# A windowed attention and a two-layer MLP on one core: the first batch taken in two parts of its tokens, the first chunk's first layer in halves, and a new order of all steps

## The chip, the core and the metric

The kernel runs on one core of one Trainium2 chip, as one program. The metric is the time on the device in microseconds (us), the median of several runs. The engines are named as the profile names them: PE (TensorE, matrix products and transposes), PEld (its weight loads), DVE (VectorE), ACT (ScalarE), POOL (GpSimd) and SP (SyncE). Each engine executes its own queue of instructions in order, and waits at an instruction until what that instruction needs is there.

## The reference

```python
# q, k, v: 8 batches x 8 heads x 576 tokens x 64, f32
scores = (1 / 8) * q @ k.transpose(0, 1, 3, 2)
rel = pos[:, None] - pos[None, :]
scores = where((rel >= 0) & (rel < 64), scores, -1e9)     # each query sees 64 keys
attn = softmax(scores)                                    # over the keys
x = (attn @ v).transpose(0, 2, 1, 3).reshape(4608, 512)   # tokens x (heads*64)
h = x @ w_in                                              # w_in 512 x 2048
g = h - tanh(h)
out = g @ w_out                                           # w_out 2048 x 512, out f32
```

## The kernel before

All products are in bf16 with sums in f32 in PSUM, which has 8 banks of 512 f32 columns over 128 partitions.

**Attention.** It is done by batch and pair of heads: pair g = 4 b + pr holds heads pr and pr + 4 of batch b. For the first batches q and k are loaded so that partition p of 96 holds tokens 6p to 6p+5 (L110). A load by POOL's queue casts to bf16 on the way; a load by SP's queue brings f32, which a cast (`ck`, `cq`, L90 on ACT) makes bf16. For each pair PE transposes k and q into a PSUM bank, in 12 matmuls of 96 columns each (`Fp` and `Ep`; L256 for batch 0, L260 for later batches) and a copy (`Fc`, `Ec`, L90 or L92) puts them into `kT` and `qp`. Scores are made for windows of 64 queries against 128 keys, in two groups of five and four windows (`Rp`, with L281 and L286 for batch 0), followed by the exponential (`Rx`, L318). For batch 0 the mask is added by PE before the scores, as a product of the identity with a tile `hide`; later pairs multiply the exponentials by a mask instead (`M`, L323 on DVE). The products with V (`P` and `PP`, L335 for batch 0) have a 65th column that gives the sums, and DVE's norm (`D`, `DS`, `DH`, and for later batches `DR`, `DN`; L377 is one of its lines) divides by them. V is held in tiles of 128 keys; the odd tiles are loaded (`LV` for batch 0, L145, and `lv`, `lt` for batch 1), the even ones are put together from halves of the odd ones by copies (`zr`, `za`, `zb`). The normalised x is turned by PE transposes (`Xp`, L397, with a copy `Xc`) or later by a DMA into chunks of 512 tokens; there are 9 chunks of tokens.

**The MLP.** Chunk c has a first layer of 16 tiles m of 128 hidden units (`H.c.m`, four matmuls of 512 columns, L431; `Hp` does some of its columns, L508), a tanh for each (`A`, L439 on ACT), the subtraction h - tanh(h) for each (`G`, L445 on DVE), and a second layer for each 128 tokens s of the chunk, in four parts of four matmuls (`W.c.s.part`, L474 and L467), with a copy and an output DMA (`O`). w_in is loaded in five blocks (`wi.0` to `wi.4`, L188) and w_out in four (`wo`), all by POOL's queue.

**Order.** Nothing is scheduled by a framework: the string `PLAN` lists all steps, and `play` runs through it word by word, so the queue of each engine has the order of the words in the string. `Fp.2.6` is "transposes of k of pair 2 into bank 6"; a last letter p, s, a or v names POOL, SP, ACT or DVE, as the engine that issues a load or executes a copy. `U.n.bank` (L227) is one filler: matmuls on a tile of constants that no result uses; 35 of them are in the string, each of 512 columns, or 384 in bank 7. `h` makes the tile `hide` and `i` the identity, both on POOL; `mt`, `mv`, `mk`, `mz` set the constant parts of tiles, and `n` and `N` make the mask and put it into PSUM.

## Time and profile before

| | |
|---|---|
| median of 3 runs | 307.93 us (307.8 to 308.22) |
| span of the profiled execution | 305.2 us |
| PE busy | 297.8 us, 98% of the span, 2599 instructions |
| DVE busy | 176.2 us, 58% |
| ACT busy | 157.5 us, 52% |
| POOL busy | 103.7 us, 34% |

The profile is of one execution, and its own time is given as its span: from the first to the last instruction that it shows. The median of the timed runs is 2.7 us longer. Rows of the timeline give the start of an instruction in us from the start of the span, its length, its engine, its line, what it writes and reads, its shape and how many like it follow. Rows of the groups give the line, the engine, the operation, the number, then busy us and mean ns of one, then the idle time of the engine just before them and what ended most of it. Rows of the DMA issues give what is loaded, the queue, the size of one and the median time from issue to landing.

### The profile page before, as it was taken

The numbers are of one execution on the slowest core, as the hardware profiler recorded it, in microseconds if no ns is written. First come the engines' busy times: TensorE is split into PE (matmuls) and PEld (weight loads), VectorE is DVE, ScalarE is ACT, GpSimd is POOL, SyncE is SP. The second block draws the span as 40 slices with busy tenths as digits, with TensorE's granted clock in tenths as the row PEclk, the third lists the DMA queues.
The fourth block names the chain that finished last, engine by engine and source line by source line (L and its number), as shares of the span: only waits on it lengthen the run. The fifth ranks groups of instructions, "written<-read, shape, count | busy, mean of one in ns | idle before, by whom it ended". The sixth has DMA issues, their size and how long they took to land.

```text
span 305.2 us, 6469 instructions
## 1 busy us (share of the span) xinstructions
PE 297.8 (98%) x2599; PEld 149.4 (49%) x2632; DVE 176.2 (58%) x316; ACT 157.5 (52%) x265; POOL 103.7 (34%) x141
## 2 busy tenths in 40 slices
...
GB/s 155 159 195 193 195 207 180 159 205 102 102 143 127 173 125 181 182 108 131 164 177 127 135 173 142 95 143 35 37 76 74 0 69 37 34 34 37 52 51 104
DMA packets 132878, 36.77 MB, mean 120 GB/s; under 512 B 119920, under 2 KB 127344, under 8 KB 132848
## 3 DMA queue, kind: packets, MB, share of 16 engines
q0 software_dynamic: 92752, 18.06, 85.3%
...
## 4 chain that ended last, share of the span: by engine, by line
PE 87%; DVE 5%; ACT 3%; issue 2%; POOL 2%; DVEq 0%; ACTq 0%; POOLq 0%
PE ps L474 38%; PE ps L431 30%; PE ps L508 6%; PE ps L348 3%; PE ps L304 2%; DVE gT L445 2%; PE ps L397 1%; ACT th L439 1%; PE ps L286 1%; PE ps L467 1%; DVE pt L323 1%; PE ps L260 1%; PE ps L281 1%; PE ps L227 1%; POOL qall L110 1%
## 5 line engine op out<-in xcount | busy, mean ns | idle before, releaser
L445 DVE TENSOR_TENSOR gT<-ps,th 128x512 bf16<-128x512 f32 x144 | 97.2, 687 | 85.3 <-ACT th L439 84.6
L474 PE MATMUL ps<-w_out_sb,gT 128*128 128x512 bf16 x527 | 131.5, 380 | 2.2 <-issue 0.8
L439 ACT ACTIVATE th<-ps 128x512 f32<-128x512 f32 x144 | 84.7, 599 | 93.0 <-PE ps L431 79.7
L431 PE MATMUL ps<-xT,wi 128*128 128x512 bf16 x496 | 120.7, 380 | 0.1
L474 PEld LDWEIGHTS <-gT 128*128 128x128 bf16 x560 | 53.3, 98 | 61.4
L431 PEld LDWEIGHTS <-wi 128*128 128x128 bf16 x496 | 47.0, 98 | 54.3
L145 POOL DMA_DIRECT2D vw<-in_v_dram x35 | 30.0, 872 | 36.1 <-PE ps L348 33.5
L90 ACT ACTIVATE ysb<-ps 128x512 f32<-128x512 f32 (+1 forms) x24 | 14.2, 593 | 30.9 <-PE ps L474 30.2
L166 POOL DMA_DIRECT2D qall<-in_q_dram x25 | 21.7, 881 | 24.1 <-DMA qw<-qall 21.4
L166 POOL DMA_DIRECT2D kall<-in_k_dram x25 | 21.7, 875 | 10.4 <-DMA kw<-kall 4.8
L314 ACT ACTIVATE pt<-ps 128x1024 bf16<-128x1024 f32 (+1 forms) x30 | 23.3, 816 | 3.5 <-PE ps L304 3.2
L323 DVE TENSOR_TENSOR pt<-pt,ps 128x1152 bf16<-128x1152 bf16 x28 | 20.5, 749 | 5.1 <-ACT pt L314 3.2
L508 PE MATMUL ps<-xT,wi 128*128 128x512 bf16 x80 | 20.8, 380 | 0.0
L92 DVE COPY ysb<-ps 128x512 f32<-128x512 f32 (+1 forms) x11 | 7.1, 650 | 20.5 <-PE ps L467 13.2
L368 DVE TENSOR_TENSOR xs<-ps,rcp 128x384 bf16<-128x384 f32 x28 | 15.2, 550 | 0.3
L318 ACT ACTIVATE pt<-ps 128x640 bf16<-128x640 f32 (+1 forms) x24 | 14.7, 659 | 0.8 <-PE ps L286 0.8
L348 PEld LDWEIGHTS <-pt 128*64 128x64 bf16 x504 | 9.4, 112 | 6.3 <-DVE pt L323 2.1
L90 ACT ACTIVATE kt<-ps 128x576 bf16<-128x576 bf16 x10 | 6.5, 647 | 10.8 <-PE ps L256 6.8
L227 PE MATMUL ps<-warm 128*128 128x512 bf16 (+1 forms) x35 | 10.6, 435 | 1.1 <-DVE warm L207 1.1
L508 PEld LDWEIGHTS <-wi 128*128 128x128 bf16 x80 | 7.4, 98 | 8.5 <-issue 0.4
L348 PE MATMUL ps<-vw,pt 128*64 128x65 bf16 x504 | 11.0, 197 | 0.3 <-DVE pt L323 0.2
L365 DVE TENSOR_TENSOR xs<-ps,rcp 128x384 bf16<-128x384 f32 x14 | 7.7, 550 | 0.1
...
## 6 DMA issues: line engine op xcount, KB each, us to landing
out_dram<-ysb SPq DMA_DIRECT2D x33, 256.0 KB, 3.1
...
kall<-in_k_dram POOLq DMA_DIRECT2D x11, 144.0 KB, 6.3
qall<-in_q_dram POOLq DMA_DIRECT2D x11, 144.0 KB, 6.6
...
```

The source lines that it names most:

```text
L90: nc.scalar.activation(o, i, ACT.Copy)
L145: nc.gpsimd.dma_start(out=w[:, 2 * i + 1, :, 0:D] if i < NF else w[64:128, 2 * i, :, 0:D], in_=v[b, :, 128 * i:128 * i + n].rearrange("h p ...
L166: nc.gpsimd.dma_start(out=token_rows(b, n)[0:c, i], in_=(q if n == "q" else k)[b, :, 128 * i:128 * i + c].rearrange("h p d -> p h d"))
L314: nc.scalar.activation(o, sp, ACT.Exp, scale=scale)
L323: nc.vector.tensor_tensor(p, p, mask.unsqueeze(1).to_broadcast([128, 2 * NJ, 64]), ALU.mult)
L348: nc.tensor.matmul(ps[r, bank, 65 * i:65 * i + 65], PT[(g + r2) % NPT][:, j, r], vw[b % 2][:, j, p0 + r2 + NP * h, :], start=True, stop=True)
L368: nc.vector.tensor_tensor(xs[b % 2][:, p0 // 2, 0:6, n // 2, :], ov[:, :, 0:D], sums[g][:, n].to_broadcast([128, 6, D]), ALU.mult)
L431: nc.tensor.matmul(hp, w_in_tile(ki, m), chunk_tile(c)[:, n.start // 64:n.stop // 64, ki % 2, 64 * (ki // 2):64 * (ki // 2) + 64], start=( ...
L439: nc.scalar.activation(th[:, n], hp, ACT.Tanh)
L445: nc.vector.tensor_tensor(gT[c][:, m, columns(s)], hp, th, ALU.subtract)
L474: nc.tensor.matmul(yp, gT[c][:, m, s * 128:(s + 1) * 128], w_out_sb[:, m, :], start=n == 1 and i == 0, stop=n == 4 and i == 3)
L508: nc.tensor.matmul(hp, w_in_tile(half + 2 * i, m), chunk_tile(c)[:, :, half, 64 * i:64 * i + 64], start=n == 1 and i == 0, stop=n == 2 and ...
```

## The change

Computation and results are meant to be the same. What differs:

- `kT` and `qp` of a pair become two halves of one tile `kq`, so that one copy (`pc`) can fill both.
- q and k of batch 0 are no longer loaded by pair, but by even pairs (0, 2) or odd pairs (1, 3) and by part of the tokens: part 0 is the first 48 partitions' worth (288 tokens), part 1 the rest, put into partitions 64 to 111. `la` loads k and `lb` loads q. Part 0 of the even pairs comes by SP in f32 and is cast (`ca`, `cb`, on ACT and DVE); the other six loads go by POOL's queue.
- Transposes (`ta`, `tb`) are by part: 12 matmuls of 48 columns. Scores (`ra`), exponentials (`rx`) and the products with V (`pp`) are by part too, part 0 being windows 0 to 3 and part 1 windows 4 to 8. The norm `pd` scales two pairs in one instruction.
- q and k of batch 1 are loaded for two pairs at a time (`l2` for k, `l3` for q), 288 KB each.
- The even tiles of V for batch 0 are put together by two copies (`zl`, `zh`) that can be placed apart.
- The first layer of chunk 0 goes in halves of 256 tokens (`I`, the "duo"): two tiles m share one bank, 8 matmuls of 256 columns, then one tanh (`J`) and one subtraction (`K`) of 512 columns for both.
- The filler is 30 matmuls instead of 35, 23 of 512 columns and 7 of 384, and none of it stands behind the first layer's start.
- There are 576 products with V instead of 584.
- The whole of `PLAN` is in a new order.

The diff, with both orders cut to their beginnings:

```diff
@@ -70,9 +70,10 @@
     vw = [const.tile([128, NJ, H, D + 1], BF16, name=f"vw{i}") for i in range(2)]
     PT_all = const.tile([128, NPT, NJ, 128], BF16, name="pt")
     PT = [PT_all[:, i] for i in range(NPT)]
-    kT = [const.tile([128, 64 + S], BF16, name=f"kt{i}") for i in range(NKR)]
+    kq = [const.tile([128, 2, 64 + S], BF16, name=f"kq{i}") for i in range(NKR)]
+    kT = [t[:, 0] for t in kq]
     kw = [const.tile([128, NP, 64 + S], BF16, name=f"kw{i}") for i in range(2)]
-    qp = [const.tile([128, S], BF16, name=f"qp{i}") for i in range(NKR)]
+    qp = [t[:, 1, 64:] for t in kq]
     qw = [const.tile([128, NP, S], BF16, name=f"qw{i}") for i in range(2)]
     q8 = [const.tile([128, NP, 64], BF16, name=f"q8{i}") for i in range(2)]
     rows_all = {n: [const.tile([128, H, E * D], BF16, name=f"{n}all{i}") for i in range(2)] for n in "qk"}
@@ -110,6 +111,95 @@
         eng.dma_start(out=t, in_=(q if n == "q" else k)[b, pr::NP].rearrange("h (p e) d -> p h (e d)", e=E))
         stage[g, n] = t
+    PART = slice(0, 48), slice(64, 112)
+    def part_source(n, odd, part):
+        src = (q if n == "q" else k)[0, odd::2].rearrange("h (p e) d -> p h (e d)", e=E)
+        return src[48 * part:48 * part + 48]
+    early = []
+    def load_part(n, odd, part, eng):
+        if eng is nc.gpsimd:
+            eng.dma_start(out=rows_all[n][0][PART[part], odd::2], in_=part_source(n, odd, part))
+            return
+        if not early:
+            t = g_pool.tile([128, M, TOK], BF16, tag="gT", name="early")
+            t = t.rearrange("p m t -> p (m t)").bitcast(F32)[:, 0:2 * 4 * E * D]
+            early.append(t.rearrange("p (n h f) -> p n h f", n=2, h=4))
+        t = early[0][PART[part], "kq".index(n)]
+        eng.dma_start(out=t, in_=part_source(n, odd, part))
+    def cast_part(n, g, part, eng):
+        t = early[0][PART[part], "kq".index(n)]
+        move(eng, rows_all[n][0][PART[part], g::NP], t[:, g // 2::2])
+    def load_two(g, n):
+        b, pr = divmod(g, NP)
+        t = rows_all[n][b % 2][0:P]
+        nc.gpsimd.dma_start(out=t[:, pr::2], in_=(q if n == "q" else k)[b, pr::2].rearrange("h (p e) d -> p h (e d)", e=E))
+        for i in range(2):
+            stage[g + 2 * i, n] = t[:, pr + 2 * i::NP]
+    def part_bank(bank):
+        t = ps[:, bank, :].bitcast(BF16)[:, 0:640].rearrange("c (n x) -> c n x", n=2)[:, :, 0:E * 48]
+        return t.rearrange("c n (e p) -> c n e p", e=E)
+    def tr_part(g, n, part, bank):
+        tp, src, r = part_bank(bank)[:, "kq".index(n)], rows_all[n][0], PART[part]
+        for e in range(E):
+            for h in range(2):
+                nc.tensor.transpose(tp[64 * h:64 * h + 64, e, :], src[r, g + NP * h, 64 * e:64 * e + 64], ident[r, r])
+    def put_part(g, part, bank, eng):
+        lo = 64 + 6 * 48 * part
+        move(eng, kq[g][:, :, lo:lo + E * 48].rearrange("c n (p e) -> c n p e", e=E),
+             part_bank(bank).rearrange("c n e p -> c n p e"))
+    def part_group(part, bank):
+        n = 4 + part
+        pair = ps[:, 4:8:3, 0:64 * n] if bank == 4 else ps[:, bank:bank + 2, 0:64 * n]
+        return pair.rearrange("p h (i t) -> p i h t", t=64), range(4 * part, 4 * part + n)
+    def scores_part(g, part, bank):
+        sp, js = part_group(part, bank)
+        n = len(js)
+        for h in range(2):
+            nc.tensor.matmul(sp[:, :, h], ident, hide[:, h].unsqueeze(1).to_broadcast([128, n, 64]),
+                             start=True, stop=False)
+        for i, j in enumerate(js):
+            for h in range(2):
+                r = slice(64 * h, 64 * h + 64)
+                nc.tensor.matmul(sp[:, i, h], kT[g][r, 64 * j:64 * j + 128], qp[g][r, 64 * j:64 * j + 64],
+                                 start=False, stop=i == n - 1)
+    def probs_part(g, part, bank):
+        sp, js = part_group(part, bank)
+        nc.scalar.activation(PT[g][:, js[0]:js[0] + len(js), :].rearrange("p i (h t) -> p i h t", h=2), sp,
+                             ACT.Exp, scale=scale)
+    def two_banks(bank):
+        return (4, 7) if bank == 4 else (bank, bank + 1)
+    def pv_part(g, part, bank):
+        for i in range(4 + part):
+            j = 4 * part + i
+            for h in range(2):
+                r = slice(64 * h, 64 * h + 64)
+                nc.tensor.matmul(ps[r, two_banks(bank)[g % 2], 65 * i:65 * i + 65], PT[g][:, j, r],
+                                 vw[0][:, j, g + NP * h, :], start=True, stop=True)
+    def norm_part(half, part, bank):
+        n = 4 + part
+        ov = ps[:, 4:8:3] if bank == 4 else ps[:, bank:bank + 2]
+        ov = ov[:, :, 0:n * (D + 1)].rearrange("p r (i c) -> p r i c", c=D + 1)
+        rc = sm_pool.tile([128, 2, 5, 1], F32, tag="rc", name="rc")
+        nc.vector.reciprocal(rc[:, :, 0:n], ov[:, :, :, D:D + 1])
+        nc.vector.tensor_tensor(xs[0][:, half, 4 * part:4 * part + n].rearrange("p w r d -> p r w d"),
+                                ov[:, :, :, 0:D], rc[:, :, 0:n].to_broadcast([128, 2, n, D]), ALU.mult)
     def load_all(b, n):
         t = rows_all[n][b % 2][0:P]
@@ -155,6 +245,12 @@
         w = vw[b % 2]
         move(eng, w[0:64, 2 * i + 2], w[64:128, 2 * i + 1])
         move(eng, w[64:128, 2 * i], w[0:64, 2 * i + 1])
+    def low_tile(i, eng):
+        move(eng, vw[0][0:64, 2 * i + 2], vw[0][64:128, 2 * i + 1])
+    def high_tile(i, eng):
+        move(eng, vw[0][64:128, 2 * i], vw[0][0:64, 2 * i + 1])
     def token_rows(b, n="k"):
         t = rows_all[n][b % 2].rearrange("p h f -> p (h f)")[:, 0:(NF + 1) * H * D]
@@ -443,6 +539,27 @@
         if c not in gT:
             gT[c] = g_pool.tile([128, M, TOK], BF16, tag="gT", name="gT")
         nc.vector.tensor_tensor(gT[c][:, m, columns(s)], hp, th, ALU.subtract)
+    def duo_mm(mp, s, bank):
+        n = columns(s)
+        hp = ps[:, bank, :].rearrange("p (m t) -> p m t", m=2)
+        for i in range(2):
+            for ki in range(4):
+                nc.tensor.matmul(hp[:, i], w_in_tile(ki, 2 * mp + i),
+                                 chunk_tile(0)[:, n.start // 64:n.stop // 64, ki % 2, 64 * (ki // 2):64 * (ki // 2) + 64],
+                                 start=(ki == 0), stop=(ki == 3))
+        hidden["duo", mp, s] = hp
+    def duo_tanh(mp, s):
+        th = sm_pool.tile([128, TOK], F32, tag="th", name="th").rearrange("p (m t) -> p m t", m=2)
+        nc.scalar.activation(th, hidden["duo", mp, s], ACT.Tanh)
+        hidden["duo", mp, s] = hidden["duo", mp, s], th
+    def duo_sub(mp, s):
+        if 0 not in gT:
+            gT[0] = g_pool.tile([128, M, TOK], BF16, tag="gT", name="gT")
+        hp, th = hidden.pop(("duo", mp, s))
+        nc.vector.tensor_tensor(gT[0][:, 2 * mp:2 * mp + 2, columns(s)], hp, th, ALU.subtract)
     def yp_bank(c, s):
         return (0, 2)[s % 2] if c == NC - 1 else (2, 0)[s % 2] if c == 0 else 2
@@ -527,6 +644,12 @@
         Fc=lambda g, k, e: put(g, "k", k, e), Ec=lambda g, k, e: put(g, "c", k, e),
         Rp=scores, Rx=probs, M=masking, za=cross_low, zb=cross_high, Z=cross_rows, zr=cross_tile,
         P=pv, D=norm, DS=norm_sums, DH=norm_half, PP=pv_pairs, DR=recip_pairs, DN=norm_pairs, Xp=x_tr, Xc=x_put, Y=x_dma,
+        la=lambda h, p, e: load_part("k", h, p, e), lb=lambda h, p, e: load_part("q", h, p, e),
+        ca=lambda g, p, e: cast_part("k", g, p, e), cb=lambda g, p, e: cast_part("q", g, p, e),
+        l2=lambda g: load_two(g, "k"), l3=lambda g: load_two(g, "q"),
+        ta=lambda g, p, k: tr_part(g, "k", p, k), tb=lambda g, p, k: tr_part(g, "q", p, k), pc=put_part,
+        ra=scores_part, rx=probs_part, pp=pv_part, pd=norm_part, zl=low_tile, zh=high_tile,
+        I=duo_mm, J=duo_tanh, K=duo_sub,
         H=first_layer, Hp=first_layer_part, A=tanh, G=subtract, W=yp_mm, O=y_out)
     def play(script):
@@ -535,89 +658,90 @@
             STEPS[what](*[ENG[a] if a in ENG else int(a) for a in args])
     PLAN = """
-        u mv.0 mv.1 lk.1.p lq.2.p LV.0.2 U.1.3 U.1.3 U.1.5 U.1.7 U.1.6 lk.3.p U.1.1 U.1.7 lk.2.p U.1.7 lq.1.p
-        lq.3.p U.4.3 LV.0.0 i lk.0.s lq.0.s U.1.3 U.1.2 U.4.0 LV.0.3 U.4.0 Ep.2.3 Fp.1.5 U.1.2 Ec.2.3.v zr.0.2.v
-        Fc.1.5.a ck.0.a mt.3 mt.1 U.1.1 U.1.3 U.1.2 U.1.4 mt.2 U.1.1 U.1.4 cq.0.a Fp.0.1 Fp.2.6 Ep.0.2 LV.0.1
-        Ep.1.3 U.1.7 Fp.3.5 Fc.2.6.a LV.0.4 lk.4.p lq.4.p h Ec.0.2.a Fc.3.5.a Ep.3.7 Ec.3.7.a Ec.1.3.v mt.0
-        Fc.0.1.v Rp.1.0.3 lk.5.p Rp.3.0.1 Rx.1.0.3 Rp.0.1.5 zr.0.3.v Rx.3.0.1 zr.0.0.v zr.0.1.v Rp.1.1.4
-        Rp.3.1.0 ck.4.v Rx.0.1.5 Rx.1.1.4 Rx.3.1.0 lq.5.p Rp.0.0.2 wi.1 wi.0 lq.6.p P.1 lv.1.1.0 lk.7.p D.1
-        Rx.0.0.2 cq.4.v Rp.2.1.0 Rp.2.0.3 Rx.2.1.0 P.0 Rx.2.0.3 P.2 Fp.4.2 ck.5.a Fc.4.2.a D.0 Ep.4.4 DS.2 P.3
-        U.1.3 lk.6.p DH.2.0 Ec.4.4.a wi.2 Xp.0.0.1.2 Fp.5.0 Xp.0.0.0.3 D.3 lv.1.0.1 lk.8.p lq.7.p U.1.4 DH.2.1
-        Xc.0.0.0.3.v Rp.4.1.5 U.1.1 lv.1.1.1 Xc.0.0.1.2.v Xp.0.1.0.7 cq.5.a Xp.0.1.1.1 Ep.5.3 Fc.5.0.a
-        Xc.0.1.1.1.v Rx.4.1.5 Hp.0.0.0 mz Xc.0.1.0.7.a ck.7.a Ec.5.3.v Hp.0.2.1 Hp.0.0.1 Rp.4.0.6 Rp.5.1.3 n
-        Hp.0.1.0 U.1.5 Hp.0.2.0 Hp.0.1.1 cq.6.v ck.6.v A.0.0 Ep.6.5 Rx.5.1.3 Rx.4.0.6 G.0.0 lv.1.0.0 A.0.2 A.0.1
-        G.0.2 wi.3 H.0.3 A.0.3 G.0.1 N U.1.7 G.0.3 lq.8.p Fp.6.3 cq.7.v Fp.7.7 Ec.6.5.a H.0.4 ck.8.a H.0.6
-        Fc.7.7.v lt.1 Fc.6.3.a A.0.4 A.0.6 H.0.5 wi.4 A.0.5 Rp.6.1.3 Rp.6.0.6 lq.9.p Rx.6.1.3 Ep.7.5 G.0.4
-        lv.1.3.1 zb.1.1.p lv.1.2.1 H.0.7 G.0.5 G.0.6 za.1.0.v Rp.5.0.3 Rx.6.0.6 A.0.7 H.0.8 H.0.9 zb.1.0.p wo.0
-        Rx.5.0.3 A.0.8 G.0.7 H.0.10 M.6 G.0.8 Ec.7.5.a A.0.9 H.0.11 za.1.1.p lv.1.3.0 A.0.10 M.5 lv.1.2.0 Fp.8.7
-        cq.8.v G.0.9 G.0.10 Rp.7.1.3 A.0.11 wo.2 Fc.8.7.a G.0.11 Rp.7.0.5 H.0.12 lk.9.p Rx.7.0.5 A.0.12 Ep.8.1
...
+        u U.6.3 U.5.4 lb.1.1.p la.1.1.p lb.0.0.s cb.2.0.a mt.2 mt.1 mz la.0.0.s ca.2.0.a mv.0 mv.1 mk cb.0.0.v i
+        lb.1.0.p lb.0.1.p mt.3 mt.0 ca.0.0.v U.1.7 U.2.0 U.1.7 ta.2.0.1 U.1.7 ta.0.0.4 U.1.5 tb.1.1.0 U.1.7
+        la.1.0.p la.0.1.p tb.0.0.4 tb.2.0.1 pc.0.0.4.a LV.0.0 LV.0.1 h U.2.7 ta.1.1.0 tb.1.0.7 tb.3.1.2 U.1.5
+        ra.0.0.5 tb.0.1.4 rx.0.0.5 pc.2.0.1.v pc.1.1.0.v LV.0.2 LV.0.3 l3.4 LV.0.4 U.1.0 tb.3.0.0 tb.2.1.3
+        ta.3.1.2 pc.3.1.2.a U.2.6 ta.1.0.7 ta.0.1.4 ta.3.0.0 ta.2.1.3 ra.2.0.1 pc.1.0.7.a wi.2 zh.1.p pc.2.1.3.v
+        zl.0.v zh.0.a pc.3.0.0.a rx.2.0.1 U.2.5 pc.0.1.4.v ra.1.0.5 rx.1.0.5 U.3.3 ra.1.1.3 rx.1.1.3 wi.0
+        pp.0.0.6 pp.1.0.6 zl.2.v zh.2.v zl.1.v pd.0.0.6 zl.3.v l2.4 cq.6.v pp.2.0.0 ra.3.0.1 ra.0.1.3 rx.3.0.1
+        wi.3 zh.3.p cq.4.p wi.1 wi.4 l2.5 rx.0.1.3 ra.3.1.5 U.1.7 pp.3.0.0 rx.3.1.5 pd.1.0.0 ra.2.1.3 pp.1.1.1
+        Xp.0.0.0.5 Ep.6.7 l3.5 n ck.4.p ck.6.p wo.2 wo.0 rx.2.1.3 Xc.0.0.0.5.a Xp.0.1.0.0 pp.0.1.1 pp.3.1.3
+        pp.2.1.3 Xc.0.1.0.0.a Ep.4.5 I.3.0.0 pd.0.1.1 I.2.0.2 Ec.4.5.a Ec.6.7.a J.3.0 J.2.0 pd.1.1.3 Xp.0.1.1.7
+        Xp.0.0.1.1 Xc.0.0.1.1.a K.3.0 Xc.0.1.1.7.v K.2.0 I.0.0.5 I.0.1.6 Fp.4.2 I.2.1.7 Fp.6.1 I.5.1.3 I.5.0.0
+        J.0.1 Fc.4.2.a K.0.1 Fc.6.1.v J.0.0 J.2.1 K.2.1 I.1.1.6 I.3.1.1 J.5.1 J.5.0 K.5.0 K.0.0 J.3.1 J.1.1
+        K.5.1 I.1.0.0 I.7.1.2 I.6.0.5 Rp.6.0.4 I.4.0.3 J.7.1 Rx.6.0.4 K.1.1 K.3.1 J.6.0 wo.1 wo.3 lv.1.3.0
+        cq.7.p lv.1.2.0 lv.1.1.1 lv.1.0.1 lv.1.0.0 lv.1.1.0 ck.7.v K.7.1 cq.5.v ck.5.v K.6.0 lk.10.p lt.1
+        lv.1.3.1 lv.1.2.1 Rp.6.1.1 Rx.6.1.1 J.1.0 K.1.0 I.6.1.4 J.4.0 K.4.0 Ep.5.2 J.6.1 Ec.5.2.a I.7.0.6
+        Rp.4.1.0 Fp.5.7 Fp.7.5 Rx.4.1.0 Fc.5.7.v K.6.1 Ep.7.3 W.0.0.2 N I.4.1.1 Ec.7.3.a J.7.0 K.7.0 Fc.7.5.v
+        W.0.1.2 Rp.5.0.4 Rx.5.0.4 Rp.7.0.5 W.0.1.0 Rp.4.0.3 W.0.0.0 J.4.1 Rx.4.0.3 Rx.7.0.5 W.0.1.1 Rp.7.1.4
+        Rp.5.1.5 W.0.0.1 W.0.0.3 W.0.1.3 Rx.5.1.5 O.0.0.a Rx.7.1.4 ck.10.a O.0.1.a za.1.3.a za.1.2.a lq.8.p
+        lk.8.p lk.9.p lk.11.p lq.9.p M.6 M.4 M.5 K.4.1 M.7 zb.1.3.p zb.1.2.p lq.11.p lq.10.p cq.8.p W.0.2.1
+        W.0.2.3 W.0.2.2 zb.1.1.v za.1.0.v za.1.1.v zb.1.0.v PP.4 DR.4 DN.4.2 DN.4.1 DN.4.0 Fp.10.1 W.0.3.0
+        W.0.2.0 PP.6 W.0.3.1 Xp.1.0.0.4 Xp.1.0.1.3 W.0.3.3 ck.8.a O.0.2.a Xc.1.0.0.4.a Fc.10.1.v DR.6 DN.6.0
+        DN.6.2 DN.6.1 Xc.1.0.1.3.a Xp.1.1.0.7 Fp.8.4 Xc.1.1.0.7.a LV.2.0 LV.2.3 LV.2.1 cq.9.p LV.2.2 Xp.1.1.1.6
+        Hp.1.1.0 Ep.8.3 Ec.8.3.a Hp.1.0.0 ck.11.v ck.9.v Xc.1.1.1.6.v Hp.1.0.1 A.1.0 Fc.8.4.v cq.11.v G.1.0
+        Hp.1.1.1 Rp.8.1.5 Rx.8.1.5 A.1.1 Fp.11.3 Fc.11.3.v cq.10.v G.1.1 W.0.3.2 H.1.3 lr.3.4 LV.3.3 lr.4.3
...
+        Fp.9.4 Ep.11.5 Ec.11.5.v G.1.3 Ep.9.6 Ep.10.7 Hp.1.2.1 Hp.1.2.0 Fc.9.4.a Ec.10.7.a Ec.9.6.v A.1.2 G.1.2
+        Z.2 Rp.10.1.2 Rp.8.0.4 H.1.6 Rx.8.0.4 Rx.10.1.2 A.1.6 G.1.6 Rp.9.0.5 Rp.11.1.4 Rx.9.0.5 H.1.5 A.1.5
+        G.1.5 H.1.4 Rp.9.1.5 A.1.4 Rx.9.1.5 Rx.11.1.4 M.8 M.9 H.1.9 H.1.8 Rp.11.0.3 PP.8 G.1.4 H.1.7 A.1.9
+        Rx.11.0.3 A.1.8 A.1.7 G.1.9 DR.8 G.1.8 DN.8.0 G.1.7 DN.8.1 DN.8.2 H.1.12 H.1.11 H.1.10 A.1.12 A.1.11
...
```

## The prediction

> **What bounds the kernel now.** I read the page first, then busy time by stretch, then the timeline of the first 23 us.

> ```profile
> span 305.2 us, 6469 instructions
> PE 297.8 (98%) x2599; PEld 149.4 (49%) x2632; DVE 176.2 (58%) x316; ACT 157.5 (52%) x265; POOL 103.7 (34%) x141
> 0.00:7.50 7.50, 6.44 (x22) 2.57 (x22) 1.33 (x5) 1.28 (x1) 6.27 (x14) 1.00 0.99 155
> 7.50:22.58 15.08, 14.63 (x315) 9.86 (x315) 10.84 (x30) 13.14 (x22) 13.23 (x22) 1.00 1.69 176
> 22.58:60.00 37.42, 37.19 (x382) 19.34 (x383) 24.13 (x49) 27.85 (x50) 28.94 (x42) 1.00 1.65 188
> 60.00:302.00 242.00, 239.54 (x1887) 117.68 (x1915) 139.68 (x233) 115.23 (x193) 55.29 (x66) 1.00 1.09 106
> ```

> The rows by stretch give the length, then busy us (and instructions) of PE, weight loads, DVE, ACT, POOL, then PE's clock, DMA share and GB/s. From 22.58 to 302 PE idles only 0.23 + 2.46 = 2.7 us. So a change of order there can win little and lose much; what can be won lies ahead of 22.58, where the first layer begins, and PE's busy time there is partly filler:

> ```profile
> 1.06 4.38 PE L227 MATMUL ps<-warm 128*128 128x512 bf16 x12 [1.06 <-DVE warm L207]
> 7.70 0.45 PE L256 MATMUL ps<-ident,qall 96*64 96x96 bf16 x12
> 7.95 0.45 PE L256 MATMUL ps<-ident,kall 96*64 96x96 bf16 x12
> 8.33 1.90 PE L227 MATMUL ps<-warm 128*128 128x512 bf16 x7
> 22.58 0.38 PE L508 MATMUL ps<-xT,wi 128*128 128x512 bf16 x1
> 57.18 1.73 PE ps L474 x8
> ```

> L227 is the filler (U); all 22 matmuls of the first stretch above are of it. In steady state one 512-column matmul takes 1.73 / 8 = 0.216 us; the first twelve fillers take 4.38. Filler ahead of 22.58 costs 6.44 (22 of them) + 1.74 (seven, 8.33 to 10.07) + about 1.0 (four single ones) = 9.2 us; two more, 0.4 by the steady row, follow. All of this is against the span, 305.2; the median of the runs, 307.93, is 2.7 longer, which lies around the span and which I leave as it is.

> **PE's own work ahead of the first layer.** A record's length holds about 0.17 of pipeline, so I take distances between starts:

> ```profile
> 13.13 0.43 PE L281 MATMUL ps<-hide,ident 128*128 128x320 bf16 x2
> 13.79 0.39 PE L281 MATMUL ps<-hide,ident 128*128 128x256 bf16 x2
> 14.11 0.29 PE L286 MATMUL ps<-qp,kt 64*128 64x64 bf16 x8
> 14.33 0.39 PE L281 MATMUL ps<-hide,ident 128*128 128x256 bf16 x2
> 18.98 0.43 PE L260 MATMUL ps<-ident,kb 96*128 96x96 bf16 x6
> 19.24 0.42 PE L260 MATMUL ps<-ident,qb 96*128 96x96 bf16 x6
> 19.59 0.51 PE L335 MATMUL ps<-vw,pt 128*64 128x65 bf16 x20
> 20.04 0.39 PE L227 MATMUL ps<-warm 128*128 128x512 bf16 x1
> 20.26 0.44 PE L397 MATMUL ps<-ident,xs 128*128 128x128 bf16 x5
> 20.54 0.42 PE L260 MATMUL ps<-ident,kb 96*128 96x96 bf16 x6
> ```

> Transposes of one tensor of one pair: 0.25 (7.70 to 7.95) or 0.26; scores of five windows 0.66 (13.13 to 13.79), of four 0.54 (13.79 to 14.33); twenty products with V 0.45; five transposes of x 0.28.

> Before, up to 22.58: 12 transpose groups of 0.26 (3.1), scores 4 x 1.20 and one group of a later pair, some 0.3 (5.1), 80 products (1.8), 18 transposes of x (1.0), together 11.0; with filler 9.2 and the start at 1.06 that is 21.3, so 1.3 of waits.

> After, up to the first duo matmul: the same scores (4.8), 72 products (1.6), 8 transposes of x (0.45), two groups of batch 1 (0.52), and 16 groups of 12 transposes of 48 columns. Half the columns could give half of 0.25, or each could cost the full 0.25 if loading weights sets it; no row has this size. I take 0.165, nearer to the half, since in the 0.25 rows pairs of transposes run side by side and columns set the distance: 2.6, between 2.0 and 4.0. Sum 10.0. Filler: eleven at the start (4.0 by the row of twelve), then 12 x 0.216 + 7 x 0.162 = 3.7; none afterwards. So 1.06 + 7.7 + 10.0 = 18.8 us without a wait.

> **When its inputs are there.** Two loads go by SP, all others by POOL's queue, in order:

> ```profile
> 1.28 0.43 SPq L110 DMA_DIRECT2D qf<-in_q_dram  x1
> qf<-in_q_dram SPq DMA_DIRECT2D x1, 288.0 KB, 3.7
> kall<-in_k_dram POOLq DMA_DIRECT2D x1, 144.0 KB, 4.9
> 1.80:4.40 2.60, 2.60 (x8) 1.06 (x7) 0.80 (x3) 0.29 (x1) 2.60 (x5) 1.00 0.99 244
> 15.30:26.20 10.90, 10.61 (x213) 6.91 (x212) 8.62 (x24) 9.86 (x17) 9.29 (x15) 1.00 1.42 195
> 10.71 0.65 POOL L110 DMA_DIRECT2D qall<-in_q_dram  x1
> qall<-in_q_dram POOLq DMA_DIRECT2D x1, 144.0 KB, 6.2
> 13.51 1.52 POOL L188 DMA_DIRECT2D wi<-in_moe_w_in_dram  x2
> wi<-in_moe_w_in_dram POOLq DMA_DIRECT2D x1, 256.0 KB, 5.8
> ```

> The load issued at 10.71 landed at 16.9, when eight q/k loads of 144 KB and V's 576 KB had come by POOL: 1728 KB. The first w_in block, issued at 13.51, landed at 19.3, after 2272 KB. In the new order the first-layer block wi.2 ends 2240 KB of POOL's loads and the batch-1 load l3.4 ends 1664 with V's tail still behind it. So wi.2 should land near 19.2 and l3.4 near 16.4. The bytes are the same; what comes forward is the identity matrix (POOL made it after eight issues, now after two) and the first 48 rows of the even pairs, so that transposes start at about 5.9 (second f32 load at 1.28 + 3.7 = 5.0, then a cast of 0.84), not 7.70. POOL gets three more casts and two V copies ahead of the w_out loads, and waits for V in the copies. Some 0.6 to 0.9 us each, they hide under the loads then in flight (wi.2, wi.0, l2.4, wi.3: 1.5 MB, over 7 us at 195 GB/s); without that cover w_out would come up to 3 us later.

> The third chain is ACT's, which makes the exps and most copies out of PSUM:

> ```profile
> 9.11 0.84 ACT L90 ACTIVATE kb<-kf 96x768 bf16<-96x768 f32 x1
> L92 POOL COPY vw<-vw 64x520 bf16<-64x520 bf16 x4 | 2.5, 620 | 2.3 <-DMA vw<-in_v_dram 2.2
> 11.46 0.65 ACT L90 ACTIVATE qp<-ps 128x576 bf16<-128x576 bf16 x1
> 13.37 3.50 ACT L318 ACTIVATE pt<-ps 128x640 bf16<-128x640 f32 x6
> 18.61 0.82 DVE L377 TENSOR_TENSOR xs<-ps,rc 128x640 bf16<-128x640 f32 x1
> 22.26 0.60 ACT L90 ACTIVATE xT<-ps 128x512 bf16<-128x512 bf16 x1
> ```

> After the two casts (to 5.9) ACT can begin pc.0.0 at about 7.4, when q of the first part is transposed. Up to the second x copy it has four copies of 0.65, one V copy (0.65 on ACT at most, by its copies of 576), eight exps of 0.58 and two x copies of 0.6: 9.1 us, so 16.5 without waits. It does wait: for the first scores about 1.5 (PE transposes the odd heads first, and POOL makes the hide mask after two V loads), for the transposes of pairs 3 and 1 about 0.5, for the scores of pair 3, which stand on PE behind three pairs' products with V, about 0.7, and for DVE's scaling pd.1.0.0 about 0.6. The copy zh.0.a waits for V's first block with a copy and seven exps behind it; 992 KB into POOL's queue, the block should be in near 12, when ACT comes to it. That gives 19.8. The two-pair scaling itself costs no more per element than 0.82 for 640, so I price it at zero; its price is that pair 0 waits for pair 1, and that lies in these waits.

> So 18.8 (PE), 19.2 (wi.2) and 19.8 (ACT and DVE) nearly coincide. I take **19.8, with 18.9 to 21.5** as bounds: 2.8 earlier than 22.58.

> **What follows the first layer's start.** Before has done more by its start: two pairs' transposes (1.04 against the 0.52 of after, whose other half is owed), one score group (0.3) and ten more transposes of x (0.55): after owes 1.3 more. It saves the later filler, 0.4. The duo steps stream the same columns: 128 of 256 for 64 of 512. No row has 256 columns with a full weight load of its own outside a change of shape; L281's 0.32 for two (13.79 to 14.11) would add 0.05 each, 6.7 us, but contains that change; the x transposes load 128 weights for every 0.055 us, so the load is covered under 128 columns already. I take zero. The chunk keeps 16 tanh and 16 subtractions, since a duo puts two output tiles of half a chunk into one bank.

> Against this, the new order leaves DVE less room in chunk 1: all of H.1.3 to H.1.15, some 17 us of PE, now run together with four masks, two scalings and the V copies. Before, the same stretch looked like this:

> ```profile
> 70.00:75.00 5.00, 5.00 (x47) 2.48 (x44) 4.81 (x9) 3.58 (x7) 0.00 (x0) 1.00 0.59 107
> L445 DVE TENSOR_TENSOR gT<-ps,th 128x512 bf16<-128x512 f32 x144 | 97.2, 687 | 85.3 <-ACT th L439 84.6
> L323 DVE TENSOR_TENSOR pt<-pt,ps 128x1152 bf16<-128x1152 bf16 x28 | 20.5, 749 | 5.1 <-ACT pt L314 3.2
> ```

> DVE was full (4.81 of 5) and PE lost nothing. Now 14 subtractions (9.6) and four masks (3.0) make 12.6 of 17 us, and the reciprocals, scalings, a copy out of PSUM and V's copies come on top, so DVE is as full as PE. I charge 0.6 for waits there and in chunk 0, between 0 and 2.5 (the whole margin of a DVE that falls one mask and two subtractions behind). From 75 us on the work is the same in another order, with little to win of 2.5 us.

> Sum: -2.8 + 1.3 - 0.4 + 0.6 = -1.3. Forecast **306.6 us**, by itself 305.3 to 307.3.

> [...] The first f32 loads moved 244 GB/s over 96 partitions, ramp included. [...]

> **Rivals.** *A load in DVE's way (slower).* The cast cq.6.v stands on DVE ahead of pd.1.0.0; it waits for l3.4, which the first layer does not need, and pd.1.0.0, its x copy and the first duo stand behind it. At 16.4 it hides (pd.1.0.0 cannot start before about 17.3). Each us of landing beyond 17.3 is a us of the end; past 19.2 the kernel is slower. L3.4 is twice as large as any q/k load of POOL before, and V's short rows lie in front of it; landing at 20.2 gives 306.6 + 2.9 = 309.5. POOL issues it near 11, so it would have to take over 8 us, where 144 KB took 4.9 to 6.2. For it: that size. Against: the count of KB. 0.18.

> *The head start is handed back.* ACT and DVE, in order, stop PE in chunks 0 and 1 by 1.9 instead of 0.6: 307.9. For it: a DVE as full as PE, and in-order copies that wait for loads. Against: before ran so at no loss. 0.18, half of it no change, half slower.

> *Narrow loads.* [...] 0.07.

> *No waits at all.* The first duo at 18.9 with no loss later: -3.7 + 0.9 = -2.8, 305.1. 0.11.

> The forecast keeps 0.46. The range, 304.6 to 309.8, leaves out some 0.06 below and 0.10 above. A measurement here can tell about 0.2%, 0.6 us. Faster by more: 0.40 of the forecast, 0.11, 0.04 of the narrow loads: 0.55. Slower: 0.18 and half of 0.18, with a little of the rest: 0.28. Same: 0.17.

> **What would show it.** Right: first transposes near 5.9, first 256-column matmul at 19 to 20.5, no filler after it, PE idle from there to 80 us under 1.5 us. Wrong: a DVE wait on q of batch 1 ahead of the scaling; the f32 loads landing past 5.6; 256-column matmuls more than 0.11 apart; PE waiting on DVE masks ahead of the products of pairs 8 and 10; the first 48-column groups at 0.25.

## The result, and the profile after

The changed kernel takes 323.08 us (median of 4 runs, 321.42 to 324.5) against 307.87 (4 runs, 307.8 to 308.22): a ratio of 1.049, with a 95% interval of 1.045 to 1.0531. The forecast was 306.6, with 304.6 to 309.8 as range: the sign was wrong and the time lies 13.3 us above the range. The spans of the profiled executions are 322.4 and 305.2. Of the four executions two ran at a mean clock of 0.984 (321.42 and 322.08 us) and two at 0.974 (324.09 and 324.5); the profile is of the one at 324.09. Each ratio here leaves out executions over 1.5% above the fastest of their kernel; the medians are of all.

The page of the changed kernel: span, busy times, and the clock in 40 slices.

```profile
span 322.4 us, 6783 instructions
...
PE 306.5 (95%) x2755; PEld 158.7 (49%) x2791; DVE 182.8 (57%) x320; ACT 150.2 (47%) x253; POOL 107.6 (33%) x146
...
PEclk9559979999999999999999999999999999999999
```

Busy time by stretch of the changed kernel, the columns as in the prediction:

```profile
0.00:9.60 9.60, 7.30 (x54) 3.03 (x54) 3.24 (x15) 2.97 (x3) 8.22 (x19) 1.00 1.05 147
9.60:23.24 13.64, 13.64 (x240) 7.30 (x236) 4.79 (x9) 5.62 (x9) 10.82 (x18) 0.50 1.97 180
23.24:43.70 20.46, 18.64 (x264) 15.25 (x263) 13.52 (x27) 13.31 (x24) 11.27 (x16) 1.00 1.34 200
43.70:47.10 3.40, 3.40 (x29) 2.30 (x26) 1.83 (x3) 2.22 (x5) 2.79 (x5) 0.50 1.31 87
...
28.00:300.00 272.00, 261.37 (x2255) 135.56 (x2287) 168.03 (x285) 133.00 (x226) 83.80 (x105) 0.99 1.05 113
```

The same view of the kernel before, from its first layer on:

```profile
22.58:300.00 277.42, 274.85 (x2247) 135.66 (x2278) 163.79 (x281) 142.26 (x242) 84.23 (x107) 1.00 1.17 117
```

Two things stand in these rows that no row of before had. The granted clock, which no row of before shows below 1.00, is 0.50 for 13.64 us ahead of the first layer and for 3.40 us in chunk 0; PE is "busy" all that time, at half speed: three 512-column fillers at 19.96 us take it 1.46, where three at 9.92 us of c1_dense, described below, at clock 1.00, take 0.82. And PE idles 272.00 - 261.37 = 10.6 us after the first layer's start, where before idled 277.42 - 274.85 = 2.6. (Some 2.2 us of either are matmuls without a record: 2755 of 2791 are in this trace, 2599 of 2632 in that of before. The trace of b3_split below, a variant of before, has all 2632 and idles 277.42 - 277.07 = 0.35 us in the same stretch.)

One thing the clock column hides. It reads 1.00 also where the trace has no record of the clock yet; the record begins at 6.18 us here and at 4.70 in the trace of before. Up to there PE was slow in both. Here are weight loads of the first fillers in the changed kernel:

```profile
1.46 0.15 PEld L323 LDWEIGHTS <-warm 128*128 128x128 bf16 x1 [0.28 <-issue]
1.89 0.15 PEld L323 LDWEIGHTS <-warm 128*128 128x128 bf16 x1 [0.28 <-issue]
...
5.73 0.15 PEld L323 LDWEIGHTS <-warm 128*128 128x128 bf16 x1 [0.28 <-issue]
6.05 0.38 PEld L323 LDWEIGHTS <-warm 128*128 128x128 bf16 x2 [0.17 <-issue]
```

They stand 0.43 us apart, twice the 0.216 us of a 512-column matmul in before's steady state. In the trace of before such loads stand 0.32 to 0.43 us apart up to 4.56. So before was at half speed too for most of its first microseconds: that is why its first twelve fillers took 4.38 us.

The timeline of the changed kernel up to the first layer (in brackets the idle time ahead and what ended it):

```profile
1.06 5.81 PE L323 MATMUL ps<-warm 128*128 128x512 bf16 x15 [1.06 <-DVE warm L303]
...
5.00 0.84 ACT L91 ACTIVATE qall<-early 48x768 bf16<-48x768 f32 x1 [2.92 <-DMA early<-in_q_dram]
...
7.21 0.84 ACT L91 ACTIVATE kall<-early 48x768 bf16<-48x768 f32 x1 [1.37 <-DMA early<-in_k_dram]
...
8.11 0.37 PE L154 MATMUL ps<-ident,kall 48*64 48x48 bf16 x12 [1.24 <-ACT kall L91]
...
28.05 0.49 PE L548 MATMUL ps<-xT,wi 128*128 128x256 bf16 x3
```

Its two f32 loads among the DMA issues (last figure: us from issue to landing):

```profile
early<-in_q_dram SPq DMA_DIRECT2D x1, 288.0 KB, 4.2
early<-in_k_dram SPq DMA_DIRECT2D x1, 288.0 KB, 5.9
```

The first layer begins at 28.05, 5.5 later than before instead of 2.8 earlier; from there to the end it is 294.35 against 282.66, 11.7 more instead of 1.5. Together 17.2, the difference of the spans. In the start, the second f32 load landed at 7.2 where 5.0 was expected, and the first transposes stand at 8.11, not 5.9. In chunk 0 the timeline shows a stop:

```profile
37.19 1.08 ACT L555 ACTIVATE th<-ps 128x512 f32<-128x512 f32 x2 [1.15 <-PE ps L548]
...
40.06 0.70 ACT L414 ACTIVATE pt<-ps 128x640 bf16<-128x640 f32 x1 [0.53 <-PE ps L382]
...
40.80 0.69 DVE L562 TENSOR_TENSOR gT<-ps,th 128x512 bf16<-128x512 f32 x1 [2.85 <-ACT pt L414]
...
42.14 0.19 PE L382 MATMUL ps<-kq 64*128 64x64 bf16 x1 [1.14 <-DVE gT L562]
...
43.00 0.27 PE L382 MATMUL ps<-kq 64*128 64x64 bf16 x7 [0.68 <-DVE gT L562]
```

The subtraction at 40.80 is `K.1.1`. Its tanh was done at 38.27, yet DVE idles 2.85 us until ACT's exponential `Rx.6.0.4` (40.06) has ended, whose result it does not use. `Rx.6.0.4` reads banks 4 and 7 by one strided access, which spans 4 to 7; `K.1.1` reads bank 6; I read in the program that `K.1.1` waits for the count that ACT raises after `Rx.6.0.4`; the trace itself shows only that it starts 0.04 us after that exponential's end. PE then waits for DVE to free a bank, twice, and the clock falls to 0.50 at 43.7.

### The profile page after: what moved, and what is told of

Its sections match the earlier page's. It is cut to its first block, busy times and chain, and to the rows that moved or that the text cites. A ratio compares the mean times of both kernels' runs of the same rounds, so it can differ in the third digit from the quotient of the medians.

```text
span 322.4 us, 6783 instructions
## 1 busy us (share of the span) xinstructions
PE 306.5 (95%) x2755; PEld 158.7 (49%) x2791; DVE 182.8 (57%) x320; ACT 150.2 (47%) x253; POOL 107.6 (33%) x146
## 4 chain that ended last, share of the span: by engine, by line
PE 64%; DMA 14%; SPq 7%; POOL 7%; DVE 4%; issue 3%; ACT 1%; POOLq 0%; ACTq 0%
PE ps L591 28%; PE ps L527 25%; DMA w_out_sb<-in_moe_w_out_dram 5%; DMA kall<-in_k_dram 4%; PE ps L625 3%; SPq L275 3%; SPq L267 3%; PE ps L444 2%; DMA xT<-xs 2%; DMA vw<-in_v_dram 2%; DMA qw<-qall 2%; PE ps L400 2%; POOL vw L235 1%; PE ps L584 1%; DVE pt L419 1%
## 5 line engine op out<-in xcount | busy, mean ns | idle before, releaser
L535 ACT ACTIVATE th<-ps 128x512 f32<-128x512 f32 x128 | 75.0, 598 | 108.5 <-PE ps L527 86.0
L527 PE MATMUL ps<-xT,wi 128*128 128x512 bf16 x444 | 107.5, 379 | 0.8 <-DVE gT L541 0.6
L527 PEld LDWEIGHTS <-wi 128*128 128x128 bf16 x444 | 42.4, 98 | 50.7 <-issue 1.1
L262 POOL DMA_DIRECT2D kall<-in_k_dram x25 | 22.0, 890 | 22.9 <-DMA kw<-kall 20.2
L91 ACT ACTIVATE ysb<-ps 128x512 f32<-128x512 f32 (+2 forms) x21 | 12.1, 576 | 24.2 <-PE ps L591 23.0
L625 PE MATMUL ps<-xT,wi 128*128 128x512 bf16 x68 | 17.3, 379 | 1.7 <-DMA xT<-xs 1.7
L548 PE MATMUL ps<-xT,wi 128*128 128x256 bf16 x128 | 16.6, 286 | 0.0
L93 DVE COPY ysb<-ps 128x512 f32<-128x512 f32 x14 | 9.6, 686 | 12.0 <-PE ps L591 12.0
L464 DVE TENSOR_TENSOR xs<-ps,rcp 128x384 bf16<-128x384 f32 x28 | 14.8, 549 | 0.2
L93 DVE COPY kq<-ps 128x576 bf16<-128x576 bf16 x12 | 9.0, 752 | 10.4 <-PE ps L154 8.1
L323 PE MATMUL ps<-warm 128*128 128x512 bf16 (+1 forms) x30 | 12.9, 560 | 1.1 <-DVE warm L303 1.1
L562 DVE TENSOR_TENSOR gT<-ps,th 128x512 bf16<-128x512 f32 x16 | 10.6, 685 | 5.8 <-ACT th L555 3.0
L414 ACT ACTIVATE pt<-ps 128x640 bf16<-128x640 f32 (+1 forms) x16 | 10.1, 651 | 7.4 <-PE ps L382 7.2
L548 PEld LDWEIGHTS <-wi 128*128 128x128 bf16 x128 | 12.6, 102 | 1.9
## 6 DMA issues: line engine op xcount, KB each, us to landing
out_dram<-ysb SPq DMA_DIRECT2D x33, 256.0 KB, 2.3
w_out_sb<-in_moe_w_out_dram POOLq DMA_DIRECT2D x4, 512.0 KB, 12.9
qall<-in_q_dram POOLq DMA_DIRECT2D x7, 144.0 KB, 5.7
```

The lines of the kernel that those rows point to most:

```text
L93: eng.tensor_copy(o, i)
L262: nc.gpsimd.dma_start(out=token_rows(b, n)[0:c, i], in_=(q if n == "q" else k)[b, :, 128 * i:128 * i + c].rearrange("h p d -> p h d"))
L527: nc.tensor.matmul(hp, w_in_tile(ki, m), chunk_tile(c)[:, n.start // 64:n.stop // 64, ki % 2, 64 * (ki // 2):64 * (ki // 2) + 64], start=( ...
L535: nc.scalar.activation(th[:, n], hp, ACT.Tanh)
L548: nc.tensor.matmul(hp[:, i], w_in_tile(ki, 2 * mp + i), chunk_tile(0)[:, n.start // 64:n.stop // 64, ki % 2, 64 * (ki // 2):64 * (ki // 2) ...
L625: nc.tensor.matmul(hp, w_in_tile(half + 2 * i, m), chunk_tile(c)[:, :, half, 64 * i:64 * i + 64], start=n == 1 and i == 0, stop=n == 2 and ...
```

## The experiments

All are timed against the kernel before on the same chip (its medians there: 307.97 to 308.4). The diffs show the words that move, cut out of their lines.

### Is it the gap in PE's work that halves the clock?

First: the idle 1.24 us ahead of the first transposes. **a1_fill** puts six fillers more at the start of the changed kernel.

```diff
-u U.6.3 U.5.4 lb.1.1.p
+u U.6.3 U.11.4 lb.1.1.p
```

> The changed kernel with six more fillers of 512 columns (1.3 us at 0.216) in the first filler group, so that PE is not idle from 6.87 to 8.11 us. Theory A (the idle 1.24 us ahead of the first transposes brought the granted clock to 0.50 from 9.8 to 23.6 us): the clock stays at 1.00 up to 40 us, the first 256-column matmul starts at 20.5 to 22.5 instead of 28.05, and the time falls by 5 to 7 us, to 316 to 318. Rival B (the late f32 loads and ACT's chain set the prologue, the clock only stretches what would have been waiting): clock 1.00 too, but the first 256-column matmul stays at 26 or later and the time falls by less than 2 us.

325.02 us, ratio 1.0554 [1.0516, 1.0592]. Its timeline, then a stretch of its busy times:

```profile
1.06 5.97 PE L323 MATMUL ps<-warm 128*128 128x512 bf16 x21 [1.06 <-DVE warm L303]
8.40 0.37 PE L154 MATMUL ps<-ident,kall 48*64 48x48 bf16 x12 [1.37 <-POOL hide L327]
```

```profile
10.69:20.93 10.24, 10.24 (x175) 5.12 (x174) 4.33 (x8) 4.79 (x8) 7.87 (x12) 0.50 2.19 176
```

The 21 fillers took hardly longer than the 15 (5.97 against 5.81), because full speed came earlier in this execution: its record of the clock begins at 3.87 us, not 6.18, and the fillers' weight loads stand 0.43 us apart only up to 3.60. So the gap stayed, and so did the half clock: a miss of both expectations, and no verdict on the gap. **b1_gap** goes the other way: the kernel before, six fillers fewer, so that it has a gap.

```diff
-U.1.3 U.1.2 U.4.0 LV.0.3 U.4.0 Ep.2.3
+U.1.3 U.1.2 U.2.0 LV.0.3 Ep.2.3
```

> The kernel before with six of its first 22 fillers taken out, so that PE is idle for about 1.5 us ahead of the first transposes at 7.70, and nothing else. Theory A (such a gap alone halves the clock for over 10 us): clock 0.50 over some 10 to 14 us, first layer's start later than 22.58 by 3 us or more, time slower by 3 to 7 us. Rival B (a gap of this length is harmless, the half clock of the changed kernel has another cause): clock 1.00, time within 0.5 us of 307.9.

307.5 us (10 runs), 0.9986 [0.9971, 1.0002]. Its timeline:

```profile
7.69 0.45 PE L256 MATMUL ps<-ident,qall 96*64 96x96 bf16 x12 [1.85 <-POOL ident L203]
8.32 1.90 PE L227 MATMUL ps<-warm 128*128 128x512 bf16 x7
```

A gap of 1.85 us, longer than the changed kernel's, and the clock of its trace is 1.00 from 3.76 us, where its record begins, to the end of PE's work; the mean clock of its ten executions is 0.999 or 1.000. The gap alone did not do it there. What b1_gap still has behind the gap is seven fillers of 512 columns. **b2_sparse** takes the eight single fillers out as well, those seven among them:

```diff
-mt.3 mt.1 U.1.1 U.1.3 U.1.2 U.1.4 mt.2 U.1.1 U.1.4 cq.0.a
+mt.3 mt.1 mt.2 cq.0.a
-Fp.1.5 U.1.2 Ec.2.3.v
+Fp.1.5 Ec.2.3.v
-Ep.1.3 U.1.7 Fp.3.5
+Ep.1.3 Fp.3.5
```

> The kernel before with the six fillers out that the gap run left out, and with the eight single fillers between 8.3 and 11.6 us out too, so that PE has little but transposes from 6.1 to 12 us. Theory A (the granted clock follows how much PE streams in stretches of 3.41 us, an idle gap of 1.8 us alone is not enough): clock 0.50 for 6.8 us or more, first layer later than 22.58 by 1.5 us or more, time slower by 1.5 to 6 us. Rival B (the half clock of the changed kernel comes from its 48-column transposes themselves, not from little work): clock 1.00, time within 0.6 us of 308.

309.17 us (10 runs), 1.0025 [1.0, 1.005]. Its busy time by stretch:

```profile
0.00:10.36 10.36, 7.40 (x46) 3.20 (x46) 3.08 (x11) 3.18 (x4) 9.13 (x18) 1.00 1.12 162
10.36:20.60 10.24, 10.24 (x153) 5.90 (x152) 4.85 (x12) 6.74 (x12) 9.29 (x16) 0.50 1.73 171
```

The kernel before now has the half clock too, from 10.36 to 20.60, with transposes of 96 columns, not 48. Its median is 1.2 us above the runs of before beside it, less than I had expected, and the interval of the ratio reaches 1.0. (The trace is of its slowest execution, 310.73 us at a mean clock of 0.983; there the first layer began at 26.02. The nine others had 0.987 to 0.994.)

What the clock went by in these runs can be worked out from their traces. Cut each of the 16 traces every 3.41 us, at times that take in those at which its clock changes (these all lie whole multiples of 3.41 us apart: 13.65, 20.48 and 3.41 in the changed kernel). For each stretch add up the columns of the matmuls that start in it, each weighted by the share of the 128 x 128 array that it uses: a filler counts 512, twelve of before's transposes (96 x 64, 96 columns) count 432, twelve of the changed kernel's (48 x 64, 48 columns) only 108. Of 1394 stretches at clock 1.00, all 19 that count under 3050 were followed by clock 0.50, and none of the 1370 over 3250; of the five between, two were. Of 42 stretches at 0.50, all 16 over 3330 were followed by 1.00, none of the 18 under 2950.

The stretch ahead of the fall counts 2116 in the changed kernel, 2204 in a1_fill and 1808 in b2_sparse. In c4_poollate, described below, it counts 2669, though the gap there is only 0.40 us and PE is busy 3.02 of the 3.41 us. In b1_gap the two stretches around its gap count 4480 and 5168. So in these traces neither the gap nor PE's busy time decided, but the columns over the array, of which twelve of the small transposes give 108 and one filler 512. In the kernel before the stretches up to 22 us count 4500 to 6864. The changed kernel's transposes of batch 0 count half as much in all, 16 times 108 against 8 times 432, and its slow stretches count 2224 to 2992, up to the last with 3532: too little for the clock to come back, though PE is busy throughout.

**c1_dense** gives the changed kernel 25 fillers more, also between the transposes:

```diff
-U.1.7 U.2.0 U.1.7 ta.2.0.1 U.1.7 ta.0.0.4 U.1.5 tb.1.1.0 U.1.7
+U.1.7 U.6.0 U.1.7 ta.2.0.1 U.3.7 ta.0.0.4 U.3.5 tb.1.1.0 U.3.7
...
```

> The changed kernel with 25 more fillers: ten ahead of the first transposes and fifteen between the groups of small transposes. The kernel before lost no clock over an idle gap of 1.8 us with seven fillers behind it, and the changed kernel with only the gap shortened did, so the idle time alone is not the cause. Theory A (the clock is set in stretches of 3.41 us by how much PE streams in them, and matmuls of 48 columns on 48 rows count for little): with filler between them the clock stays at 1.00 up to 40 us, the first 256-column matmul starts at 22.5 to 24.5 instead of 28.05 although 5 us of filler were added, and the time falls by 3.5 to 5.5 us, to 317.5 to 319.5. Rival B (density does not matter; the clock falls as before, or ACT's chain holds the start): first 256-column matmul at 26.5 or later, time 321 to 325.

325.94 us (321.32 to 326.51), 1.0482 [1.0354, 1.0609]. In the profiled execution, 325.6 us, the clock is at 1.00 from the start of its record up to 43 us, but the first layer begins at 26.91, only 1.1 earlier. A stretch of it, then its timeline:

```profile
10.36:20.60 10.24, 9.68 (x222) 5.37 (x221) 3.45 (x7) 4.59 (x8) 9.48 (x15) 1.00 1.86 180
```

```profile
8.72 0.37 PE L154 MATMUL ps<-ident,kall 48*64 48x48 bf16 x12
...
26.91 0.27 PE L548 MATMUL ps<-xT,wi 128*128 128x256 bf16 x1
```

The clock part of the theory held, its price did not: from the first transposes to the first layer it is 18.2 us, against 19.9 in the changed kernel, since the fillers between the transposes take PE time themselves and the first transposes come 0.6 later behind those ahead of them. The rest took 297.0 us, 2.6 more than in the changed kernel, with two stretches of half clock, at 43 and at 163 us; the execution at a mean clock of 1.000 is the one that took 321.32.

### The order of the words in chunks 0 and 1

**a2_kword** moves one exponential behind two subtractions.

```diff
-Rx.6.0.4 K.1.1 K.3.1 J.6.0
+K.1.1 K.3.1 Rx.6.0.4 J.6.0
```

> The changed kernel with the subtractions K.1.1 and K.3.1 named ahead of the exponential Rx.6.0.4 instead of behind it; the queue of each engine keeps its order, only what waits for what can change. Theory A (K.1.1 started at 40.80, just when this exponential ended at 40.76, though its tanh had ended at 38.27: it waits for an exponential that it does not need, and PE then waits for banks): DVE's idle 2.85 us ahead of K.1.1 is gone, PE's idle time from 40 to 44 us falls from 2.2 to under 0.6, no second stretch at clock 0.50 near 44 to 47 us, time 319 to 320.5. Rival B (DVE would wait anyway, for the batch-1 casts ck.7 and cq.5 behind it): PE idle there above 1.5, time 322 to 323.

321.26 us, 1.042 [1.0384, 1.0455]. The stretch of the stop in the changed kernel:

```profile
40.00:44.00 4.00, 2.18 (x24) 1.64 (x23) 3.20 (x7) 1.99 (x4) 1.99 (x3) 0.97 1.88 159
```

The same in a2_kword, where this work stands some 2 us later, and DVE's timeline there (PE is busy up to 46 us too):

```profile
40.00:44.00 4.00, 4.00 (x51) 3.17 (x50) 3.44 (x7) 2.79 (x6) 1.24 (x2) 1.00 1.80 175
```

```profile
40.35 1.29 DVE L562 TENSOR_TENSOR gT<-ps,th 128x512 bf16<-128x512 f32 x2 [0.35 <-ACT th L555]
```

DVE's wait fell from 2.85 to 0.35, PE is busy throughout, the second half clock is gone, and the time from the first layer to the end is 289.68, 4.7 less. (The median gained 1.8 only: in its profiled run the first half clock lasted 17.07 us and the first layer began at 30.09.)

**c2_order** adds four like moves: `Rp.7.0.5` ahead of `Rx.5.0.4`; `K.4.1` out from behind three masks; two of these masks, `M.6` and `M.4`, ahead to where their exponentials are; `Rx.7.1.4` ahead of the copy `O.0.0`.

```diff
-Rp.5.0.4 Rx.5.0.4 Rp.7.0.5 W.0.1.0 Rp.4.0.3 W.0.0.0 J.4.1 Rx.4.0.3 Rx.7.0.5
+Rp.5.0.4 Rp.7.0.5 Rx.5.0.4 W.0.1.0 Rp.4.0.3 W.0.0.0 J.4.1 K.4.1 M.6 Rx.4.0.3 M.4 Rx.7.0.5
-Rx.5.1.5 O.0.0.a Rx.7.1.4
+Rx.5.1.5 Rx.7.1.4 O.0.0.a
-M.6 M.4 M.5 K.4.1 M.7
+M.5 M.7
```

> The changed kernel with words of the order moved between 37 and 62 us and nothing else: K.1.1 and K.3.1 ahead of Rx.6.0.4; Rp.7.0.5 ahead of Rx.5.0.4; K.4.1 right behind J.4.1; the masks M.6 and M.4 ahead of Rp.7.1.4, M.5 and M.7 where they were; the copy O.0.0 behind Rx.7.1.4. Theory A (after the first layer's start, the time is lost to DVE and ACT instructions that stand, or wait for PSUM banks, behind work that they do not need): from the first 256-column matmul to the end it takes 285.5 to 288 us instead of 294.35 (289.7 with the two subtractions alone), whatever the clock does ahead of it; time 314.5 to 318.5. Rival B (DVE is full there, so moving only shifts the waits): 289 or more, time 319 to 322.

318.54 us, 1.0331 [1.0253, 1.0408]; first layer at 28.23, and 288.61 from there: 5.7 less than in the changed kernel. Its stretches, the first to be set beside 16.88 busy in the changed kernel:

```profile
50.00:70.00 20.00, 19.65 (x244) 10.95 (x242) 15.39 (x30) 12.45 (x23) 13.78 (x18) 1.00 1.26 131
28.00:300.00 272.00, 267.52 (x2319) 137.42 (x2317) 170.73 (x288) 135.26 (x231) 84.35 (x105) 1.00 1.05 113
```

In this trace no matmul lacks its record, so its idle 4.5 us stands against some 10.6 - 2.2 = 8.4 in the changed kernel: 3.9 of waits, and half of the 3.4 us at clock 0.50, make 5.6 of the 5.7. **c3_both** is c2_order with c1_dense's fillers.

> The extra filler and the moved words together. If both theories hold, their gains add, since they lie in different stretches: first 256-column matmul at 22.5 to 24.5, 285.5 to 288 us from there, time 310 to 314. If the rest of the kernel waits for loads that come at fixed times (w_out's last block at 42.4, V of batch 1 up to 48), an earlier start is eaten and the time is 315 to 318.

317.52 us, 1.0293 [1.0207, 1.0378]; first layer 27.59, the rest 286.24.

```profile
28.00:300.00 272.00, 269.69 (x2322) 138.21 (x2321) 172.40 (x289) 135.62 (x231) 83.75 (x105) 1.00 1.06 113
```

With the clock at 1.00 the rest is still 3.6 longer than before's. PE idles 2.3 us in it, all matmuls on record, where b3_split idled 0.35: that is 2.0, the owed work of the forecast is 0.9, and 0.7 stays open. The start did not gain as expected (22.5 to 24.5).

### Why the f32 loads land late

**a3_ports** puts q's f32 part into partitions 64 to 111, k's into 0 to 47.

```diff
-t = early[0][PART[part], "kq".index(n)]
+t = early[0][PART[n == "q"], "kq".index(n)]
```

> The changed kernel with the f32 load of q, part 0, put into partitions 64 to 111 instead of 0 to 47 (the cast moves it back), so that the two f32 loads go into different partitions. Theory A (two loads into the same 48 partitions are slow, which made the second land at 7.19 where the second of before landed at 4.93): the second lands at 5.7 or earlier, first transposes at 6.7 or earlier, no idle gap over 0.4 us, no half clock, time 314 to 317. Rival B (it is slow because POOL's casting loads share the DMA engines, and the partitions do not matter): it lands at 6.8 or later and the time stays at 322 to 324.

323.27 us, 1.0469 [1.0414, 1.0524]; they landed at 4.75 and 7.17 (5.0 and 7.2 in the changed kernel). That both go into the same 48 partitions is not it; each load by itself still spans 48. **c4_poollate** has POOL make its three constant tiles ahead of its first loads, so that these come later:

```diff
-u U.6.3 U.5.4 lb.1.1.p la.1.1.p lb.0.0.s
+u U.6.3 U.5.4 i h n lb.1.1.p la.1.1.p lb.0.0.s
...
```

> The changed kernel with POOL making the identity and both masks first, so that its first loads go out some 2 us later; a look at the f32 loads of SP, which landed at 4.98 and 7.19 where those of before landed at 3.97 and 4.93. Theory A (POOL's casting loads share the DMA engines with them): the second f32 load lands at 5.7 or earlier, the first transposes start at 6.8 or earlier. Rival B (something of the loads themselves, such as 48 partitions by four heads, makes them slow): it lands at 6.8 or later.

323.96 us (one run); landings 5.29 and 6.81, first transposes 7.73, first layer 26.37. POOL's loads are not the cause either. The queues' traffic agrees: from 2 to 3 us SP's loads move 0.26 MB in before and in the changed kernel, but from 3 to 4 us 0.29 in before and 0.15 in the changed kernel, and 0.14 in c4_poollate, where POOL's queue moves nothing in that time. **b3_split** loads the f32 rows of the kernel before in halves of 48 partitions, the size of the new parts:

```diff
+for r in (slice(0, 48), slice(48, 96)):
+    eng.dma_start(out=t[r], in_=src[r])
```

> The kernel before with each of its two f32 loads over 96 partitions issued as two loads over 48 partitions each; a look at their landings, which were at 3.97 and 4.93. Theory A (a transfer that spans 48 partitions moves its bytes slower, as it took until 7.19 for the same bytes in the changed kernel): the last of the four lands at 6.2 or later. Rival B (the span does not matter; four heads in one transfer, or the address, does): it lands at 5.6 or earlier, the extra issues being 0.9 us of SP's time.

307.45 us (one run). Its DMA issues:

```profile
kf<-in_k_dram SPq DMA_DIRECT2D x2, 144.0 KB, 2.7
qf<-in_q_dram SPq DMA_DIRECT2D x2, 144.0 KB, 3.9
```

The last half landed at 6.03 where before's second load landed at 5.0, but it was issued at 2.20 and not at 1.28. That lies between what either theory gave. **d2_swap** loads k first, which PE transposes first.

```diff
-lb.0.0.s cb.2.0.a mt.2 mt.1 mz la.0.0.s ca.2.0.a
+la.0.0.s ca.2.0.a mt.2 mt.1 mz lb.0.0.s cb.2.0.a
```

> The changed kernel with SP's two f32 loads, and the casts behind them, in the other order: k first, then q. Theory A (both are slow for their span of 48 partitions, and what lands last is the second, whichever it is): first 4.8 to 5.3, second 6.6 to 7.5. Rival B (k's addresses are slow): the first lands at 6 or later, the second by 7.

321.82 us (one run). The second load is the slow one whichever tensor it is (its landing 6.81), the first transposes start at 6.72 and the first layer at 24.78. Its DMA issues:

```profile
early<-in_k_dram SPq DMA_DIRECT2D x1, 288.0 KB, 4.4
early<-in_q_dram SPq DMA_DIRECT2D x1, 288.0 KB, 5.5
```

### A stop of PE that waits for nothing

d2_swap, at full clock until 16.2, showed a stop amid 48 like transposes, with no releaser. Its timeline, then the stretch up to the stop:

```profile
12.38 0.64 PE L154 MATMUL ps<-ident,kall 48*64 48x48 bf16 x45
14.98 0.21 PE L154 MATMUL ps<-ident,kall 48*64 48x48 bf16 x3 [1.96 <-issue]
```

```profile
0.00:12.90 12.90, 11.84 (x223) 6.02 (x224) 4.98 (x17) 4.98 (x7) 10.99 (x22) 1.00 1.37 148
```

Up to it PE had issued 223 matmuls and 224 weight loads. c1_dense and c3_both stop after the same 223 and 224, a2_kword too. In d3_best and e1_all, below, it is the same count. If it is the count that matters, the stop comes at that count wherever it falls. **e2_count** is d2_swap with each filler cut into pieces of 128 columns, so that the count is reached sooner.

```diff
-nc.tensor.matmul(ps[:, bank, 0:128 * w], warm, ...)
+for s in range(w):
+    nc.tensor.matmul(ps[:, bank, 128 * s:128 * s + 128], warm, warm, ...)
```

> The changed kernel with k's f32 load first and each filler of 512 or 384 columns issued as four or three fillers of 128, the same columns in all. In the look with the loads swapped PE stopped for 2.0 us at 12.82, behind its 448th recorded instruction, within the transposes of k ahead of ra.2.0.1, waiting for nothing. Theory A (PE had used up the instructions that were loaded, since the small transposes need so many): with some 90 more fillers PE stops at about the same count, 448, and so some steps earlier, between 8.5 and 11 us, and not at that step. Rival B (the step waits for data or a bank): it stops at the same transposes, at a count over 550.

326.36 us (one run). The same two views:

```profile
11.61 0.46 PE L154 MATMUL ps<-ident,qall 48*64 48x48 bf16 x23
14.78 0.20 PE L154 MATMUL ps<-ident,qall 48*64 48x48 bf16 x1 [2.71 <-issue]
```

```profile
0.00:12.00 12.00, 10.94 (x223) 9.82 (x224) 4.65 (x17) 4.22 (x5) 10.62 (x22) 1.00 1.49 142
```

The stop moved from k's transposes to q's and from 12.9 to 12.0, and stands after 223 and 224 again, 2.71 us instead of 1.96. So it goes with the count of instructions, not with the step. The count alone is not enough: the kernel before reaches it at 17.7 us, at full clock, and idles less than 0.2 us there. What makes PE stop there, the supply of instructions or something else, no run here shows. It stopped for 0.6 to 2.7 us in seven runs, six of them at full clock up to there. The trace of the changed kernel itself, at half clock there, shows no such stop, so the stop is no part of its loss; it takes the place of some of the half clock when that is mended.

### All together

**d3_best**: c2_order's words, c4_poollate's constants, and more filler only ahead of the scores `ra.2.0.1` (that behind is taken out).

> The changed kernel with all that has helped so far: the moved words, POOL's identity and masks first, and filler only ahead of ra.2.0.1 (none behind it). If the prologue is bound by PE at full clock: clock 1.00, first 256-column matmul at 24 to 25.5, 286 us from there, time 312 to 314.5, so still slower than before, by the late f32 loads and by the 0.9 us more work that it owes. If it is bound by loads and copies: first 256-column matmul at 26 or later, time 315 to 318.

318.34 us, 1.0335 [1.0262, 1.0408]. A miss, with the first layer at 27.78: the clock fell later, for 6.83 us. The stretch ahead of the fall counts 2288: no filler stands in it, and PE's stop, here of 1.23 us, does.

```profile
18.94:25.77 6.83, 5.89 (x90) 2.97 (x88) 4.30 (x11) 3.19 (x5) 4.57 (x8) 0.50 1.33 202
```

**e1_all**: c2_order's words and d2_swap's loads, no filler added.

> The changed kernel with the moved words and with k's f32 load ahead of q's, no filler added. If the causes are independent: first 256-column matmul at 23 to 25 where the clock stays high up to 16 us, as in the look with the loads swapped, 285.5 to 288.5 us from there, time 311.5 to 315.5. If they hide one another (the earlier start meets w_out or V of batch 1 not yet there): 290 or more from the first layer's start, time 316 or more. In both cases slower than before.

315.87 us (312.36 to 317.69), 1.0267 [1.0227, 1.0308], the best of all, still slower than before. The profiled run is its fastest, 312.36, with the clock at 1.00; the first layer begins at 22.79 and the rest is 287.87; the others, at a mean clock of 0.989, took 315.82 to 317.69. Its timeline, then PE's waits after the first layer's start (line, what it waited for, us in total, times, longest):

```profile
14.43 0.21 PE L154 MATMUL ps<-ident,kall 48*64 48x48 bf16 x3 [1.20 <-issue]
```

```profile
PE ps L625 <- DMA xT<-xs: 1.6, 1, 1.6
PE ps L400 <- DMA qw<-qall: 1.1, 1, 1.1
```

So with order and loads mended, and in an execution whose clock stays up, the first layer starts where before's does, the stop included. Of the 5.2 us that the rest still has over before's 282.66, 2.7 are these waits for DMA transposes, between 130 and 170 us, and 0.9 is owed work; 1.6 stay open.

## Why the prediction was wrong

**The start, 19.8 forecast and 28.05 measured.** Its PE terms held in part: in e1_all, at full clock, the scores took 4.7 us (4.8 taken) and the products 1.6 (1.6), but the 16 groups of transposes 3.5 (2.6 taken; about 0.30 for a group by itself, 0.15 to 0.25 each where several follow one another) and the 15 fillers among them 3.7 (3.0 by its prices). wi.2 landed at 20.29 (19.2 taken), l3.4 at 17.81, before the 19.2 from which a load in DVE's way would have made the kernel slower. What failed:
- *"second f32 load at 1.28 + 3.7 = 5.0"*: 7.2, and with it 2.2 on the first transposes. The narrow-loads rival (0.07, and 0.04 in the sum of the chances) pointed at these loads; no run shows the price that it took, and what the runs showed in its place is a second load that lands 2.2 later. a3_ports put the two into different partitions and they landed at 4.75 and 7.17, but each by itself still spans 48 partitions, so what that costs it does not show. What makes these loads slow is open: neither POOL's loads nor that they share 48 partitions nor the tensor; b3_split did not decide.
- *The clock* is in no term. From the first transposes to the first layer took 19.94 at half clock, 15.87 in e1_all at full clock, 13.9 in the forecast: some 4.1 for the clock. The other 2.0 are the stop of 1.2 in e1_all and the transposes and fillers above. I counted filler as 9.2 us of PE time to be saved, and never asked what it holds up; all rows of before read 1.00, so no rival had it. Yet the sign was in a row that I used: the first twelve fillers at 4.38 us, 0.365 each against 0.216, ran at half clock for the most part.

**From the first layer on, +1.5 forecast and +11.7 measured.** The step that failed is *"I charge 0.6 for waits there and in chunk 0, between 0 and 2.5"*: PE's idle time rose by 8.1, with 1.7 for the second half clock. The owed work (1.3 - 0.4 = 0.9) and the 256-column matmuls at no extra cost (16 of them in 1.75 us, 0.109 apart) stood; some 1.0 us I can't assign. I bounded the waits by DVE's throughput, "one mask and two subtractions behind". But DVE wasn't full: in the 20 us from 50 on it was busy 9.78 us in the changed kernel, and PE 16.88; c2_order's moves of words made that 15.39 and 19.65. What cost was order: instructions that wait in a queue for another engine's, with others behind them that could go. These moves, which change no work, took away half of the 11.7, and this is shown. That the particular wait of `K.1.1` comes from two reads whose spans of banks overlap is read from the program's waits and not shown by a run; the move shows that the wait costs.

*The rival "the head start is handed back"* had direction and mechanism right, at 1.9 instead of some 10. *"No waits at all"* and *"a load in DVE's way"* did not happen. By my own list of what would show it wrong, the f32 loads past 5.6, PE idle above 1.5 us ahead of 80 us (5.2), and the first groups of 48 columns at 0.25 or more (0.30) came true.

Not settled: the waits of 0.4 to 3.0 us on DMA transposes at 130 to 170 us, which differ from variant to variant and were not tried by themselves; in a1_fill, c1_dense and e2_count a half clock of 3.41 us follows on them.
